# Exchanging the row sums of squares through small SBUF transfers in a fused attention and mixture kernel

## The chip, the cores and the metric

The kernel runs on one core of one Trainium2 chip. The metric is the device time of one execution in microseconds. Three executions of the kernel before took 2057.47, 2061.39 and 2066.37 us; the median is 2061.39 us. The profile was taken on a further execution of 2060.28 us, whose span from the first to the last instruction is 2058.4 us.

## The reference

```python
def _attn_ref(q, k, v):                       # B, H, S, D = 4, 8, 576, 64
    scores = scale * np.matmul(q, k.transpose(0, 1, 3, 2))
    # heads 0..3: the last 32 positions; heads 4..7: every 4th of the last 128
    masks = np.stack([mask_plain if h < H // 2 else mask_dil for h in range(H)], axis=0)
    scores = np.where(masks[None, :, :, :], scores, -1000000000.0)
    ...                                       # softmax over the keys
    return np.matmul(attn, v)

def _moe_ref(x, w_gate, w_val, w_out, rms_g):  # 2304 tokens, 512 -> 1536 -> 512
    rms = np.sqrt(np.mean(x * x, axis=-1, keepdims=True) + 1e-06)
    xn = x / rms * rms_g
    g = xn @ w_gate
    silu = g * (1.0 / (1.0 + np.exp(-g)))
    val = xn @ w_val
    return (silu * val @ w_out)

def _moe2_ref(x, w_gate, w1, w2):              # 8 experts, 512 -> 1024 -> 512
    ...                                       # P: Sinkhorn-normalised gate, 2304 x 8
    for e in range(E):
        h = np.maximum(x @ w1[e], 0.0)
        out += P[:, e:e + 1] * (h @ w2[e])
```

The output of the attention (8 heads of 64) is one row of 512 values per token, and the first step of the second part divides that row by its root mean square.

## The kernel before

**Stages.** The kernel has two phases. In the first (up to about 610 us) the attention and the gated feed-forward layer run together; in the second the eight experts do, with matrix products in which seven block products stand for eight. TensorE works in split precision: every operand is kept as a high and a low part, and each product takes three passes (`PASSES`).

**Attention tiles.** The 2304 tokens are handled in 20 attention tiles of up to 128 tokens, five to a batch. `att_tile` is a generator: it issues a stretch of instructions at each step and yields between them. A tile has the scores (psS), the softmax, a transpose (psT), the product with the values (psX), the scaling into `xf` (named xs in the rows), the sums of squares `ssq`, the normalisation and a last transpose (psXT) from which `xn`, the input of the feed-forward layer, is written as high and low part.

**Two orders of tokens.** Heads 0 to 3 (group 0) use a plain window, heads 4 to 7 (group 1) every fourth position, so in a tile the 128 partitions hold the tokens of the two groups in two orders: partition u of group 1 holds the token that partition `32*(u%4) + u//4` of group 0 holds, counted within each group. A token's row sum needs both halves, so each half sum has to be brought to the other half's partition. In the kernel before two matmuls with permutation matrices (`perms`) do this at L286 into the PSUM tile psR; DVE adds the two halves and 1e-6 into `rstd` (L288), POOL raises it to -0.5 (L289), and DVE scales both halves of the row with it (L291).

**Blocks and pacing.** The feed-forward layer goes by eight blocks of 256 or 320 tokens, each with the tiles of the same tokens (two or three). Per block and chunk, `gemm_h` makes the products pg and pv (L472) and from them h (L484 to L487: ACT, DVE, ACT, POOL), and `gemm_out` the product po (L442), added into `partial` (L451, L453). From block 2 on, `spread` mixes three streams: the products of block i with 34 steps; the attention of block i+1 (`block_att`), for which seven steps per tile are counted; and `weight_sums`, which loads blocks of the experts' weights into three buffers (kbd, vbd, conv; L667), forms sums on POOL and DVE (L680 to L688) and stores them (L690). Tiles 0 to 4 are done earlier with sets of buffers of their own; from tile 5 on `rows` is true, and tiles share one set. Then psT, psR, psXT use one PSUM bank (tag "single").

**Order.** Each engine carries out its own instructions strictly in the order in which a scheduler placed them when the kernel was built; the steps above are hints to it. SP issues nearly all transfers in one such order; ACT issues the loads of q, k and v. Each DMA signals one of eight completion semaphores, taken in turn, and the next user of a semaphore waits until the DMA that had it before has landed.

The lines that the change touches:

Of the kernel before, what the change touches and what calls it, by code (L numbers as in the profile page):

```python
# [7 lines left out]
F32 = mybir.dt.float32  # L8
# [8 lines left out]
P = 128  # L17
# [12 lines left out]
def attention_moe_kernel(  # L30
# [14 lines left out]
    nc = tc.nc  # L45
# [12 lines left out]
    ps_a = psum_a.enter_context(tc.tile_pool(name="ps_a", bufs=3, space=bass.MemoryType.PSUM))  # L58
# [11 lines left out]
    apool = ph1.enter_context(tc.tile_pool(name="apool", bufs=1))  # L70
# [5 lines left out]
    perms = cst[:, C_PM:C_G].rearrange("p (v k) -> p v k", v=2)  # L76
# [78 lines left out]
    def att_tile(n, xn, c0, bufs, after_qk=None, after_pv=None):  # L155
# [4 lines left out]
        rows = bufs.rows  # L160
# [9 lines left out]
        for hp in range(4):  # L170
            for g in range(4):
                off = hp * 160 + 32 * g if hp < 2 else ((hp - 2) * 4 + g) * 64
                if rows:
                    for s in range(2):
# [3 lines left out]
                            lhsT=qs[half, hp, g, :],  # L178
                            rhs=bufs.k[hp // 2][half, 0, off : off + 64],
                            start=True,  # L180
                            stop=True,
# [5 lines left out]
                    lhsT=qs[:, hp, g, :],  # L187
                    rhs=bufs.k[hp // 2][:, :, off : off + 64],
                    start=True,
                    stop=True,  # L190
# [27 lines left out]
        single = dict(tag="single", bufs=1) if rows else dict(tag="a", bufs=3)  # L218
# [15 lines left out]
        for hp in range(4):  # L234
            vals = bufs.v[hp // 2].rearrange("p s (a g d) -> p s a g d", a=2, g=4)
            for g in range(4):
                if rows:
                    for s in range(2):
# [3 lines left out]
                            lhsT=pt[half, hp * 128 + 32 * g : hp * 128 + 32 * g + 32],  # L242
                            rhs=vals[half, 0, hp % 2, g, :],
                            start=True,
                            stop=True,
# [5 lines left out]
                    lhsT=pt[:, hp * 128 + 32 * g : hp * 128 + 32 * g + 32],  # L251
                    rhs=vals[:, :, hp % 2, g, :],
                    start=True,
                    stop=True,
# [20 lines left out]
        ssq = apool.tile([P, 2], F32, tag="ssq", name=f"ssq_{n}", bufs=2)  # L275
# [5 lines left out]
        if after_pv:  # L281
            after_pv()
        yield
        psr = ps_a.tile([P, 512], F32, name=f"psR_{n}", **single)
        for j in range(2):
            nc.tensor.matmul(psr[:, j : j + 1], lhsT=perms[:, j, :], rhs=ssq[:, 1 - j : 2 - j], start=True, stop=True)  # L286
        rstd = apool.tile([P, 2], F32, tag="rstd", name=f"rstd_{n}", bufs=2)
        nc.vector.scalar_tensor_tensor(out=rstd, in0=psr[:, 0:2], scalar=1e-6, in1=ssq, op0=ALU.add, op1=ALU.add)  # L288
        nc.gpsimd.tensor_tensor(out=rstd, in0=rstd, in1=neghalf, op=ALU.pow)  # L289
# [478 lines left out]
    blocks = []  # L768
# [5 lines left out]
    def block_att(i):  # L774
        tok0, n, tl = blocks[i]

        def xn():
            if i not in xns:
                xns[i] = mpool.tile([P, 4, 2, n], F32R, tag=f"xn{i % 2}", name=f"xn_{i}", bufs=1)
            return xns[i]  # L780

        for tn, c0 in tl:
            more = tn + 1 < 20
            yield from att_tile(
                tn, xn, c0, set0,
                (lambda: set0.load_qk(tn + 1, nc.scalar)) if more else None,
                (lambda: set0.load_v(tn + 1, nc.scalar)) if more else None,
            )
# [47 lines left out]
    def some(g, n):  # L836
        for _ in range(n):
            yield next(g, None)

    def tail():  # L840
        for _ in range(9):
            yield
        yield from x_load(0)
        yield from x_split(0)
        yield from first_weights(0)
# [41 lines left out]
    for i in range(2, 8):  # L887
        sides = [(some(sgen1, 24), 24)]
        if i < 7:
            sides.append((block_att(i + 1), 7 * len(blocks[i + 1][2])))  # L890
        else:
            sides += [(tail(), 34)]
        spread(moe1_chunks([(i, 0), (i, 1), (i, 2)]), 34, sides)
# [210 lines left out]
    n = len(units)  # L1104
# [127 lines left out]
```

## Time and profile before

| | |
|---|---|
| median of three executions | 2061.39 us |
| the profiled execution | 2060.28 us |
| its span | 2058.4 us |
| outside the span | 1.9 us |
| PE busy | 2002.0 us (97%) |
| DVE, ACT, POOL busy | 1375.8, 1097.3, 1216.1 us |
| tiles 5 to 19, first and last permutation matmul | 120.2 and 526.7 us |

PE stands for TensorE's matmuls and PEld for its weight loads; DVE is VectorE, ACT ScalarE, POOL GpSimd, and SPq the queue of SyncE, which only issues transfers. A row of a timeline gives the start in the span, the length, the engine, the line and what is written from what; an idle time before it and what ended that stands in brackets. PE is busy almost without a gap, so every instruction on it counts, and what another engine does counts only where PE ends up waiting.

### The profile page before, as it was taken

The numbers are of one execution on the slowest core, as the hardware profiler recorded it, in microseconds if no ns is written. First come the engines' busy times: TensorE is split into PE (matmuls) and PEld (weight loads), VectorE is DVE, ScalarE is ACT, GpSimd is POOL, SyncE is SP. The second block draws the span as 40 slices with busy tenths as digits, with TensorE's granted clock in tenths as the row PEclk, the third lists the DMA queues.
The fourth block names the chain that finished last, engine by engine and source line by source line (L and its number), as shares of the span: only waits on it lengthen the run. The fifth ranks groups of instructions, "written<-read, shape, count | busy, mean of one in ns | idle before, by whom it ended". The sixth has DMA issues, their size and how long they took to land.

```text
span 2058.4 us, 42667 instructions
## 1 busy us (share of the span) xinstructions
PE 2002.0 (97%) x16122; PEld 1966.2 (96%) x16122; DVE 1375.8 (67%) x2890; ACT 1097.3 (53%) x2418; POOL 1216.1 (59%) x1198
## 2 busy tenths in 40 slices
PE   6899999999999999999999999999999999999999
PEld 4788999999998999999999999999999999999999
DVE  7985444434347898778777676776776567667666
ACT  5665443334347666666665555555555654555453
POOL 4786555655647668778776455455545544554452
PEclk9999999999999999999999999999999999999999
DMA  9423767776555678887799656666677666666652
GB/s 271 167 83 113 252 217 240 236 239 225 201 203 211 250 254 283 299 294 265 283 326 352 197 197 227 215 200 226 222 243 266 222 208 200 181 198 205 203 177 81
DMA packets 206557, 459.95 MB, mean 223 GB/s; under 512 B 16784, under 2 KB 56464, under 8 KB 206352
## 3 DMA queue, kind: packets, MB, share of 16 engines
q1 hardware_dynamic: 199296, 438.25, 62.4%
q10 hardware_dynamic: 7056, 18.98, 3.1%
q8 instruction: 127, 2.08, 0.4%
q14 instruction: 78, 0.64, 0.1%
HBM read 344.44 MB, written 112.72 MB: 222 GB/s over the span
## 4 chain that ended last, share of the span: by engine, by line
PE 74%; DMA 7%; DVE 7%; POOL 5%; issue 4%; ACT 2%; SPq 1%; DVEq 0%; POOLq 0%; ACTq 0%
PE ya L1057 17%; PE pa L1004 17%; PE yb L1057 9%; PE pb L1004 9%; PE po L442 4%; PE pc L1004 4%; PE yc L1057 4%; PE pv L472 4%; PE pg L472 4%; DMA kbd<-in_w 1%; DMA sums<-kbd 1%; DMA w0r<-in_w 1%; DMA w0s<-sums 1%; POOL w_s L712 1%; DMA sums<-conv 1%
## 5 line engine op out<-in xcount | busy, mean ns | idle before, releaser
L712 POOL TENSOR_TENSOR w_s<-w0s,w_s 128x512 fp32r<-128x512 f32 x192 | 260.5, 1359 | 92.9 <-ACT w_s L711 91.3
L983 POOL TENSOR_TENSOR h_s<-p,h_s 128x384 fp32r<-128x384 f32 x96 | 104.8, 1113 | 322.6 <-ACT h_s L982 273.7
L1093 DVE SCALAR_TENSOR_TENSOR acc<-ya,Pm,acc 128x256 f32<-128x256 f32 x510 | 221.9, 478 | 65.3 <-PE ya L1057 65.2
L712 POOL TENSOR_TENSOR w_a<-w0r,w_a 128x512 fp32r<-128x512 f32 x144 | 195.3, 1359 | 110.8 <-ACT w_a L711 110.3
L1004 PE MATMUL pa<-x_t,w_s 128*128 128x384 f32 x1152 | 224.1, 336 | 1.9 <-ACT p L1016 1.9
L1057 PE MATMUL ya<-w_t,h_s 128*128 128x256 f32 x1728 | 224.5, 282 | 0.9 <-ACT acc L1082 0.9
L1057 PEld LDWEIGHTS ya<-w_t,h_s 128*128 128x128 f32 x1728 | 218.8, 190 | 1.3 <-ACT acc L1082 1.2
L1004 PEld LDWEIGHTS pa<-x_t,w_s 128*128 128x128 f32 x1152 | 197.1, 188 | 2.5 <-ACT p L1016 2.1
L472 PE MATMUL pv<-xn,w_v 128*128 128x320 f32 (+1 forms) x1152 | 182.2, 301 | 9.7 <-ACT hf L484 2.4
L472 PE MATMUL pg<-xn,w_g 128*128 128x320 f32 (+1 forms) x1152 | 184.2, 301 | 3.2 <-DVE hf L485 1.5
L442 PE MATMUL po<-h,w_o 128*128 128x320 f32 (+1 forms) x1152 | 175.7, 301 | 7.0 <-DVE partial L453 2.4
L472 PEld LDWEIGHTS pv<-xn,w_v 128*128 128x128 f32 x1152 | 162.7, 191 | 14.4 <-ACT hf L484 4.1
L711 ACT CAST w_s<-w0s 128x512 fp32r<-128x512 f32 x192 | 119.8, 625 | 105.4 <-PE pb L1004 65.6
L1093 DVE SCALAR_TENSOR_TENSOR acc<-yb,Pm,acc 128x256 f32<-128x256 f32 x258 | 109.7, 476 | 93.4 <-PE yb L1057 93.3
L442 PEld LDWEIGHTS po<-h,w_o 128*128 128x128 f32 x1152 | 159.8, 190 | 11.2 <-DVE partial L453 3.8
L472 PEld LDWEIGHTS pg<-xn,w_g 128*128 128x128 f32 x1152 | 162.7, 190 | 7.0 <-DVE hf L485 2.3
L487 POOL TENSOR_TENSOR h<-hf,h 128x256 fp32r<-128x256 f32 (+1 forms) x96 | 80.1, 835 | 111.7 <-ACT h L486 111.2
L983 POOL TENSOR_TENSOR h_s<-r,h_s 128x384 fp32r<-128x384 f32 x96 | 96.5, 1028 | 69.1 <-ACT h_s L982 52.9
L1057 PE MATMUL yc<-w_b,h_a 128*128 128x256 f32 x864 | 122.4, 282 | 0.0
L1057 PE MATMUL yb<-w_t,h_s 128*128 128x256 f32 x864 | 121.1, 281 | 0.1
L1057 PE MATMUL yb<-w_t,h_a 128*128 128x256 f32 x864 | 120.2, 282 | 0.0
L711 ACT CAST w_a<-w0r 128x512 fp32r<-128x512 f32 x144 | 89.4, 622 | 56.0 <-DMA w0r<-in_w 15.8
(250 smaller groups left out, 4722.9 us busy)
## 6 DMA issues: line engine op xcount, KB each, us to landing
w_t<-split SPq DMA_DIRECT2D x128, 512.0 KB, 4.3
w0r<-in_w SPq DMA_DIRECT2D x96, 512.0 KB, 6.1
w0s<-sums SPq DMA_DIRECT2D x96, 512.0 KB, 7.3
w_b<-split SPq DMA_DIRECT2D x96, 512.0 KB, 3.9
split<-w_t SPq DMA_DIRECT2D x64, 512.0 KB, 3.0
split<-w_b SPq DMA_DIRECT2D x48, 512.0 KB, 4.0
w1r<-in_w SPq DMA_DIRECT2D x32, 512.0 KB, 5.6
w1s<-sums SPq DMA_DIRECT2D x32, 512.0 KB, 7.6
```

Source lines behind the costliest of these rows:

```text
L442: nc.tensor.matmul(po[:, :n], lhsT=ow[f][:, a, dc * P : dc * P + P], rhs=hs[blk, f][:, bb, :n], start=k == 0, stop=k == 11,)
L472: nc.tensor.matmul(ps[:, :n], lhsT=w[kt, fg][:, a, fo * P : fo * P + P], rhs=xn[:, kt, bb, :n], start=k == 0, stop=k == 11,)
L487: late_g = nc.gpsimd.tensor_tensor(out=h[:, 1, :n], in0=hf, in1=h[:, 0, :n].bitcast(F32), op=ALU.subtract)
L711: nc.scalar.copy(v[:, :, 0, :], src)
L712: lo_eng.tensor_tensor(out=v[:, :, 1, :], in0=src, in1=v[:, :, 0, :].bitcast(F32), op=ALU.subtract)
L983: eng.tensor_tensor(out=h[:, 1, :], in0=src, in1=h[:, 0, :].bitcast(F32), op=ALU.subtract)
L1004: nc.tensor.matmul(ps, lhsT=w1s[u, a][:, kt, hl, q * P : q * P + P], rhs=xc[b, kt][:, xl, :TH], start=fresh and k == 0, stop=k == 5, skip_ ...
L1057: nc.tensor.matmul(ps, lhsT=hh[u, a, q][:, hl, jj * P : jj * P + P], rhs=w2s[u, b][:, q, wl, :], start=fresh and k == 0 and jj != 1, stop= ...
L1093: nc.vector.scalar_tensor_tensor(out=dst, in0=ps, scalar=scale, in1=dst, op0=ALU.mult, op1=ALU.add)
```

## The change

From tile 5 on the two matmuls on PE are left out. In their place a tile `ssx` in SBUF is filled by eight transfers from SP: each carries 32 values of 4 bytes, from every fourth partition to 32 partitions in a row, or back. The addition on DVE reads `ssx` in place of PSUM. `att_tile` yields twice more, so that more of the other streams is placed between the transfers and the addition, and the pacing counts nine steps per tile in place of seven. Tiles 0 to 4 keep the matmuls.

```diff
@@ -281,9 +281,19 @@
         yield
-        psr = ps_a.tile([P, 512], F32, name=f"psR_{n}", **single)
-        for j in range(2):
-            nc.tensor.matmul(psr[:, j : j + 1], lhsT=perms[:, j, :], rhs=ssq[:, 1 - j : 2 - j], start=True, stop=True)
+        if rows:
+            psr = apool.tile([P, 2], F32, tag="ssx", name=f"ssx_{n}", bufs=2)
+            for a in range(4):
+                nc.sync.dma_start(psr[a:P:4, 0:1], ssq[32 * a : 32 * a + 32, 1:2])
+                nc.sync.dma_start(psr[32 * a : 32 * a + 32, 1:2], ssq[a:P:4, 0:1])
+            yield
+            yield
+        else:
+            psr = ps_a.tile([P, 512], F32, name=f"psR_{n}", **single)
+            for j in range(2):
+                nc.tensor.matmul(
+                    psr[:, j : j + 1], lhsT=perms[:, j, :], rhs=ssq[:, 1 - j : 2 - j], start=True, stop=True
+                )
         rstd = apool.tile([P, 2], F32, tag="rstd", name=f"rstd_{n}", bufs=2)
@@ -887,7 +897,7 @@
         if i < 7:
-            sides.append((block_att(i + 1), 7 * len(blocks[i + 1][2])))
+            sides.append((block_att(i + 1), 9 * len(blocks[i + 1][2])))
```

Line numbers after the change are higher by 10 behind the new lines. The order of the instructions differs from the kernel before only in the stretch of tiles 5 to 19. Three places show what moves.

SP while tile 15 is handled, before; DMAHW0 to DMAHW7 are the completion semaphores of transfers, Pool, DVE and Activation those of the engines:

```order
L690 DMA sums_9_103<-kbd 128x1024 [waits DMAHW2_49,Pool_49]
L690 DMA sums_9_103<-vbd 128x1024 [waits DMAHW3_49,Pool_49]
L667 DMA kbd<-in_w 128x2x512 [waits DMAHW2_49]
L667 DMA vbd<-in_w 128x2x512 [waits DMAHW6_49,DMAHW3_49]
L690 DMA sums_9_119<-conv 128x1024 [waits DMAHW7_49,DVE_49,Pool_49]
```

The same place after; L287 and L288 are the eight new transfers of this tile:

```order
L288 DMA ssx_5683<-ssq_5646 32x1 [waits DMAHW3_49,Activation_49]
L288 DMA ssx_5683<-ssq_5646 32x1 [waits DMAHW4_49]
L700 DMA sums_9_103<-kbd 128x1024 [waits DVE_49,Pool_49]
L287 DMA ssx_5683<-ssq_5646 32x1 [waits DMAHW6_49,Activation_49]
L700 DMA sums_9_103<-vbd 128x1024 [waits DMAHW7_49,DVE_49,Pool_49]
L287 DMA ssx_5683<-ssq_5646 32x1 [waits DMAHW0_49]
L287 DMA ssx_5683<-ssq_5646 32x1 [waits DMAHW1_49]
L677 DMA kbd<-in_w 128x2x512 [waits DMAHW5_49,DMAHW2_49]
L288 DMA ssx_5683<-ssq_5646 32x1 [waits DMAHW3_49]
L287 DMA ssx_5683<-ssq_5646 32x1 [waits DMAHW4_49]
L288 DMA ssx_5683<-ssq_5646 32x1
L700 DMA sums_9_119<-conv 128x1024 [waits DMAHW6_49,DVE_49,Pool_49]
```

The stores of the weight sums and the next load of kbd now stand behind transfers that wait for ACT's sums of squares of tile 15, and three of the eight transfers stand behind the load.

PE at the start of block 3 (tile 9 is the last of its tokens), before:

```order
L442 MATMUL po_2_3_3665<-h_11_3509,w_o_1886 128x256 x3
L286 MATMUL psR_3327<-ssq_3300,cst 128x1 x2
L176 MATMUL psS_3535<-kbd,q_3227 32x64 x32
L604 MATMUL pl_3759<-xn_2200,wg 16x256 x7
L297 MATMUL psXT_3370<-cst,xs_3298 128x128 x4
L604 MATMUL pl_3759<-xn_2200,wg 16x256
L472 MATMUL pg_0_3515<-xn_2793,w_g_383 128x320
```

The same place after:

```order
L452 MATMUL po_2_3_3695<-h_11_3539,w_o_1886 128x256 x3
L176 MATMUL psS_3565<-kbd,q_3251 32x64 x32
L614 MATMUL pl_3798<-xn_2206,wg 16x256 x8
L641 MATMUL ptl_3890<-id_83,lg_3845 128x16 x2
L641 MATMUL ptl_3890<-id_83,lg_3845 64x16
L307 MATMUL psXT_3419<-cst,xs_3305 128x128 x4
L482 MATMUL pg_0_3545<-xn_2811,w_g_383 128x320
```

The permutation is gone, and the last transpose of the tile still stands directly ahead of the first product of the block, with one more matmul of the gate and its small transposes (ptl) ahead of it.

PE at the start of block 5 (tile 14 is the last of its tokens), before:

```order
L297 MATMUL psXT_5234<-cst,xs_5168 128x128 x4
L472 MATMUL pg_10_5314<-xn_3881,w_g_1719 128x256
L472 MATMUL pg_10_5314<-xn_3881,w_g_1738 128x256 x3
...
L472 MATMUL pv_11_5348<-xn_3881,w_v_1812 128x256 x3
L472 MATMUL pg_0_5379<-xn_4677,w_g_383 128x320 x3
```

The same place after:

```order
L482 MATMUL pv_11_5408<-xn_3935,w_v_1812 128x256 x3
L176 MATMUL psS_5459<-kbd,q_5153 32x64 x32
L452 MATMUL po_2_0_5522<-h_8_5240,w_o_1830 128x256 x2
...
L452 MATMUL po_2_3_5589<-h_11_5433,w_o_1886 128x256 x3
L307 MATMUL psXT_5313<-cst,xs_5207 128x128 x4
L614 MATMUL pl_5692<-xn_3935,wg 16x256 x6
L482 MATMUL pg_0_5439<-xn_4725,w_g_383 128x320
```

The last transpose moved from 40 matmuls ahead of the block's first product to only the gate's six ahead of it, and 47 of the 48 matmuls of po were pulled in front of both. The start of block 7 (tile 19) changed in nearly the same way.

## Rows read from the trace of the kernel before

**Rows 1.** The page: its first line and PE's busy time.

```profile
span 2058.4 us, 42667 instructions
PE 2002.0 (97%) x16122; PEld 1966.2 (96%) x16122; DVE 1375.8 (67%) x2890; ACT 1097.3 (53%) x2418; POOL 1216.1 (59%) x1198
```

**Rows 2.** Busy times by stretch: length, PE, PEld, DVE, ACT, POOL, clock, DMA.

```profile
110.00:560.00 450.00, 438.52 (x4896) 421.00 (x4895) 220.99 (x472) 192.21 (x442) 283.62 (x384) 1.00 0.61 204
300.00:350.00 50.00, 49.88 (x526) 48.26 (x526) 17.79 (x39) 17.75 (x40) 28.64 (x38) 1.00 0.72 241
```

**Rows 3.** PE's waits, 110 to 560 us: total us, times, longest.

```profile
PE psXT L297 <- DVE xs L291: 2.5, 4, 0.9
PE po L442 <- DVE partial L453: 2.4, 3, 1.3
...
PE po L442 <- POOL h L487: 0.3, 1, 0.3
```

**Rows 4.** The tile psR, 110 to 560 us: ns min/median/max.

```profile
L286 PEld LDWEIGHTS psR<-ssq,cst x60: 187/192/193, 120.1 to 526.7; 128*128 128x128 f32 x60
L286 PE MATMUL psR<-ssq,cst x60: 166/250/250, 120.2 to 526.7; 128*128 128x1 f32 x60
```

**Rows 5.** Timeline at the permutation of tile 19: start, length.

```profile
526.32 0.53 PEld L286 LDWEIGHTS psR<-ssq,cst 128*128 128x128 f32 x4
...
526.78 0.30 PEld L442 LDWEIGHTS po<-h,w_o 128*128 128x128 f32 x2
```

**Rows 6.** Timeline of SP, two runs of three transfers: start, length.

```profile
998.71 1.29 SPq L548 DMA_DIRECT2D xr<-x2d  x3
...
938.00 2.24 SPq L548 DMA_DIRECT2D xr<-x2d  x3
```

**Rows 7.** DMA issues in short windows: KB, median us from issue to landing.

```profile
x2d<-partial SPq DMA_DIRECT2D x1, 160.0 KB, 1.8
...
sums<-kbd SPq DMA_DIRECT2D x1, 512.0 KB, 5.1
x2d<-partial SPq DMA_DIRECT2D x1, 160.0 KB, 4.8
...
id<-in_consts SPq DMA_DIRECT2D x1, 1.0 KB, 3.0
...
sums<-conv SPq DMA_DIRECT2D x1, 512.0 KB, 4.5
```

**Rows 8.** Timelines at the start of block 3, with tile 9.

```profile
262.47 0.34 SPq L690 DMA_DIRECT2D sums<-conv  x1
...
262.49 0.19 ACT L278 ACTIVATION_READ_ACCUMULATOR psX<-xs 128x1 f32 x1
...
265.39 0.16 DVE L288 SCALAR_TENSOR_TENSOR rstd<-psR,ssq 128x2 f32<-128x2 f32 x1
...
267.33 0.63 PE L297 MATMUL psXT<-cst,xs 128*128 128x128 f32 x4 [0.34 <-DVE xs L291]
...
268.31 0.42 PE L472 MATMUL pg<-xn,w_g 128*128 128x320 f32 x1 [0.24 <-ACT xn L307]
```

**Rows 9.** Timeline of PE ahead of block 5, with tile 14.

```profile
394.52 0.60 PE L297 MATMUL psXT<-cst,xs 128*128 128x128 f32 x4
...
399.76 1.92 PE L472 MATMUL pg<-xn,w_g 128*128 128x320 f32 x12
```

**Rows 10.** POOL's waits for transfers, 300 to 350 us: total us, times, longest.

```profile
POOL vbd L685 <- DMA vbd<-in_w: 3.6, 1, 3.6
```

**Rows 11.** Timelines of SP, ACT and POOL while tile 15 is handled.

```profile
412.70 0.38 SPq L690 DMA_DIRECT2D sums<-kbd  x1
...
415.86 0.38 SPq L667 DMA_DIRECT2D kbd<-in_w  x1
...
417.83 0.44 ACT L484 ACTIVATE hf<-pg 128x320 f32<-128x320 f32 x1 [0.97 <-PE pg L472]
...
425.48 0.72 POOL L685 TENSOR_TENSOR kbd<-kbd 128x256 f32<-128x256 f32 x1
```

## The prediction

> **What bounds the kernel now.** I read the page first: PE is busy for 2002.0 of 2058.4 us, so over the whole program PE is the bound [rows 1]. The change reaches tiles 5 to 19 only, so the busy times of that stretch come next: between 110 and 560 us PE is busy for 438.52 of 450 us [rows 2]. PE idles there for 11.5 us in all, and that is everything that better timing could win beside the work taken off PE itself. The waits of PE in that stretch name its parts: the last transpose of a tile, psXT, waits for the scaling on DVE 4 times for 2.5 us together; po waits 2.4 us for the adding on DVE; for h from POOL it waits only 0.3 us [rows 3]. The other engines have room on average: DVE is busy for 221 and POOL for 284 of the 450 us [rows 2]. How late they may be before PE feels it is told by one wait: between 300 and 350 us POOL stood 3.6 us waiting for a load of vbd [rows 10], and PE still was busy for 49.88 of 50 us [rows 2].
>
> **What is removed.** There are 60 weight loads and 60 matmuls of psR for 15 tiles, so four pairs per tile [rows 4]. Their durations (192 and 250 ns) overlap, so I don't add them up; I take the distance by which they hold up the stream. At tile 19 the first weight load of psR starts at 526.32 and the next weight load of po at 526.78 [rows 5]: 0.46 us. For 15 tiles that is 15 x 0.46 = 6.9 us, all on PE, where nothing hides it. This term is the surest. A second gain comes with the new order: psXT of tiles 7, 12 and 17 now stands among the products of a later f, some 5 us of matmuls further back. Of the 2.5 us for which psXT waited [rows 3], 0.34 us belong to tile 9 [rows 8] and stay; the other three waits, 2.2 us, go. Together 9.1 us.
>
> **What is added on SP.** Eight transfers per tile, 120 in all. Issuing them takes time on SP: three transfers of xr in a row took 1.29 us, and in another place 2.24 us [rows 6], so 0.43 to 0.75 us each, and 3.4 to 6.0 us for eight. No transfer as small as these 128 bytes stands in the trace. Their landing I bound by others: 1.8 us for 160 KB with nothing ahead of it, 4.8 us for the same 160 KB issued 0.4 us behind a store of 512 KB that itself took 5.1 us, and 3.0 us for 1 KB in the early, busy stretch [rows 7]. From the sums of squares to the last landing that makes 5.2 us (3.4 + 1.8) to 10.8 us (6.0 + 4.8). I take 7 us, nearer to the low end: the issues nearest in kind are the quick ones, and the landing near 3 us is that of the smallest transfer.
>
> The second pair in these rows also shows that a small transfer does not overtake a large one that was issued just ahead of it: it landed with it. The Trainium skill says the same (DMA: Bandwidth & Descriptors, Queues, rings and completion order): on each DMA engine the descriptors of one queue are consumed in the order of the ring. By that rule alone every tile whose transfers stand directly behind a load of 512 KB would be at the long end for landing; the trace agrees in its one pair. The same page (Anatomy of one DMA) puts the fixed cost of a transfer at about 2 us, whatever its size; eight in a row overlap it, so by that figure the estimate would be 3.4 + 2.0 = 5.4 us. No run here shows it for 128 bytes.
>
> **Where this is late: PE.** In most tiles the new order leaves room: two yields more put several products between the sums and the addition. The starts of blocks 3, 5 and 7 are the exceptions, since the first product there needs the last tile's psXT.
>
> Block 3, tile 9: ACT ends the sums of squares at 262.68 (262.49 + 0.19), and the addition ran at 265.39; from it to psXT took 1.94 us [rows 8]. With 7 us the addition comes at about 269.7, 4.3 us later than before. The two ends give 2.5 and 8.1 us. Part of this is covered: the gate's matmul and its small transposes that now precede psXT, and what PE had been waiting there anyway (0.34 and 0.24 us) come to about 0.8 us. The store of conv ahead, issued at 262.47 and 4.5 us in landing [rows 7, 8], also holds a completion semaphore that one of the last two transfers needs, so before 267.0 they can't all be issued; the low end is therefore no likelier than the middle. I take 3.5 us of PE idle, with 1.7 to 7.3 as the ends.
>
> Blocks 5 and 7, tiles 14 and 19: before, psXT ran 5.2 us ahead of the block's first product (394.52 against 399.76) [rows 9], so that ACT's and DVE's work behind it was hidden. Now it is not: I charge 1 us each, the distance from psXT to the first product in block 3 (268.31 - 267.33) [rows 8]. In front of it stand the matmuls of po with two PSUM buffers, and the addition for rstd stands ahead of the first adding of po on DVE; a DVE that waits for the transfers therefore holds the third po up. I charge 1.5 us each for that, between nothing and 3 us. Both together: 5 us, ends 2 and 8.
>
> **Where this is late: DVE, POOL and SP.** Elsewhere DVE, which can't pass the waiting addition, stands still for up to some 3 us; behind it are hf and partial, and PE waits for these in the end. The 3.6 us of POOL's wait that PE did not feel [rows 2, 10] are the measure: I cost a stall up to this size at nothing. On SP the transfers stand ahead of stores and loads of the weight sums. The worst place is tile 15: the store of kbd went out at 412.70; now it stands behind two transfers that need sums of squares made around ACT's hf at 417.83, so it leaves 5 to 6 us later, and so does the load of kbd (before at 415.86), which waits for the store's landing. From that load's issue to POOL's use of it at 425.48 lie 9.6 us [rows 11]; with a landing of 4.5 to 5.1 us, as such transfers took [rows 7], some 4.8 us of it are room, so POOL starts about 1 us late, still below the 3.6 us [rows 10]. Tile 10 has the same pattern with less delay. For the partly hidden stalls of tiles 8, 10, 11, 13, 15, 16 and 18 I charge 0.4 us each, 3 us; the ends are 0 and 2 us each, 14 us. In tile 5 the transfers stand ahead of five loads of weights, on which ACT starts only when it is through with the blocks of weights before them; I cost this at nothing, and at up to the 3.4 to 6.0 us of the eight issues if that cover is gone.
>
> **The sum.** -6.9 - 2.2 + 3.5 + 5 + 3 = +2.4 us. On the profiled execution of 2060.28 us (span 2058.4 us and 1.9 us around it, which do not change) this is 2062.7 us. That execution stood 1.1 us below the median of 2061.39 us, so I predict **2063 us**. All low ends together (1.7 + 2 + 0) give -5.4, all high ends (7.3 + 8 + 14) +20.2, that is 2056 to 2082 us.
>
> **Rivals.** First, *the transfers are hidden everywhere* and only the gain is left: -9.1 us, 2052 us. For it speaks the slack of PE against late engines [rows 2, 10]; against it that psXT of tile 9 stands directly ahead of the block's first product, and that even 5.2 us are 2.5 us too long there. It also cannot reach much further down, for the idle time of the stretch is 11.5 us and most of it has nothing to do with this change.
>
> Second, *SP becomes the bound of the weight sums* (slower). Its place is SP's order: eight issues and their waits for semaphores delay the load that follows by 3.4 to 6.0 us at each tile, and POOL already stands waiting for such loads. It decides from the point where POOL is held up by more than the 3.6 us that PE did not feel. Then h comes late, and PE waits at po for POOL, which it did for 0.3 us only [rows 3]. If the 13 tiles from 7 on each cost PE 2 us beyond the gain, the sum is 13 x 2 - 9.1 + 3.5 = +20 us, 2082 us. For it: SP issues everything in one order, and the transfers at the long end need 10.8 us. Against it: the weight sums are only needed in the second phase, and each wait that PE does not feel costs nothing.
>
> Third, *the saved PE time is not real*, because PE waits at the same places anyway: the gain is then about nothing, and the cost of block starts stays, +11 us, 2073 us. Against it: PE waits for 11.5 us in this stretch, mostly not near a permutation.
>
> **How the numbers follow.** This kernel's executions differ by about 0.25% either way, and changes of up to 0.5% (10.3 us, so 2051.1 to 2071.7 us) can't be told from none. The forecast case, 2056 to 2071 us, gets 0.57; the hidden case 0.13, half of which may be measured below 2051 us; SP as the bound 0.24 and the lost saving 0.06, which lie above 2071.7 us except for a few hundredths. So faster 0.07, same 0.62, slower 0.31. The range for 8 in 10 is 2053 to 2083 us; it leaves out a good part of the hidden case and the far end of the second rival. The likeliest case's own range is 2056 to 2071 us.
>
> **What the profile after would show.** The psR rows from tile 5 on are gone and PE's matmuls are fewer by 60. SP shows eight issues per tile, in 3.4 to 6.0 us where nothing else stands between them, and a landing near 3 us. At the start of block 3 PE idles 3 to 4 us ahead of psXT and its first product; at the starts of blocks 5 and 7 PE idles about 2 us each. PE's waits for psXT at tiles 7, 12 and 17 are gone, and po's wait for h from POOL stays below 3 us. I am wrong on the side of too slow if psXT of tile 9 comes without a gap, and on the other if PE's waits for h and hf grow to 10 us or more, or if an issue of a 128-byte transfer takes over 0.75 us.

## The result and the profile after

The changed kernel takes 2090.34 us (median of 4 runs, 2088.14 to 2092.18) against 2061.4 us of the kernel before beside it: ratio 1.0145, interval 1.0129 to 1.016, some 29 us slower. I had predicted 2063 us with a range of 2053 to 2083, so the time lies outside the range. A per cent is 20.6 us here; where a run below is given in us against the kernel before, it is its ratio times that.

The page after, its first line and PE's busy time, answers to [rows 1]:

```profile
span 2089.1 us, 42738 instructions
PE 2011.3 (96%) x16062; PEld 1974.2 (95%) x16062; DVE 1385.8 (66%) x2890; ACT 1097.6 (53%) x2418; POOL 1216.7 (58%) x1198
```

The span grew by 30.7 us. PE has 60 matmuls fewer and is still busy 9.3 us longer; its idle time grew by the other 21.4 us. If the removed matmuls took the 6.9 us that I charged, the remaining work took 16 us longer than before in this trace. Both parts lie in the stretch of [rows 2]; the columns are the same (length, PE, PEld, DVE, ACT, POOL, granted clock, DMA):

```profile
110.00:560.00 450.00, 417.99 (x4651) 399.18 (x4634) 213.16 (x449) 183.90 (x420) 264.22 (x358) 0.96 0.58 193
300.00:350.00 50.00, 49.32 (x512) 47.95 (x511) 18.35 (x38) 16.03 (x34) 28.54 (x38) 1.00 0.73 240
```

PE's busy time over 450 us fell from 438.52 to 417.99 us, and the mean granted clock from 1.00 to 0.96. The second row shows that it is not so everywhere: from 300 to 350 us, the block of two tiles, PE is busy for 49.32 of 50 us, against 49.88 before.

PE's waits in that stretch (total us, times, longest), answering to [rows 3], and DVE's first wait:

```profile
PE psXT L307 <- DVE xs L301: 13.9, 8, 4.2
PE ptl L641 <- ACT lg L634: 3.2, 1, 3.2
PE po L452 <- DVE partial L463: 3.0, 2, 2.2
PE psS L176 <- ACT psX L278: 2.7, 1, 2.7
...
PE po L452 <- ACT h L496: 1.8, 1, 1.8
PE pv L482 <- ACT hf L494: 1.8, 2, 1.5
...
PE po L452 <- POOL h L497: 0.4, 1, 0.4
```

```profile
DVE rstd L298 <- DMA ssx<-ssq: 49.2, 12, 7.3
```

The largest new wait is that of psXT, 13.9 us against 2.5, and behind it stands DVE: the addition for rstd waits 12 times for the transfers, 49.2 us in all. PE's wait for h from POOL, the sign of my rival of SP as the bound, is 0.4 us against 0.3 before.

The transfers by themselves (ns of an issue min/median/max; the last row is us from issue to landing):

```profile
L288 SPq DMA_DIRECT2D ssx<-ssq x60: 492/592/1373, 117.7 to 565.2; - x60
L287 SPq DMA_DIRECT2D ssx<-ssq x60: 469/592/1522, 119.7 to 564.5; - x60
DMA to landing us min/median/max: 1.6/3.0/7.0
```

An issue takes 0.59 us and a landing 3.0 us, both as I had assumed. What was longer is the way from the sums to the last landing. The timeline of ACT, SP and DVE at tile 13 is the longest of them:

```profile
388.74 0.19 ACT L278 ACTIVATION_READ_ACCUMULATOR psX<-xs 128x1 f32 x1
...
397.02 0.36 ACTq L125 DMA_DIRECT2D q<-in_qt  x1
...
397.91 0.40 ACT L496 CAST h<-hf 128x256 fp32r<-128x256 f32 x1 [7.68 <-DMA ssx<-ssq]
```

```profile
393.33 0.38 SPq L677 DMA_DIRECT2D vbd<-in_w  x1
393.81 0.50 SPq L288 DMA_DIRECT2D ssx<-ssq  x1
...
398.18 0.59 SPq L288 DMA_DIRECT2D ssx<-ssq  x1
```

```profile
SPq L677 <- DMA sums<-vbd: 5.7, 1, 5.7
```

The sums are there at 388.93, but SP stands at a load of vbd ahead of the transfers until 393.33: for 5.7 us it waits until the store from the same buffer has landed (the single row, SP's waits from 386 to 400 us). Its eight issues then end at 398.77, and DVE's addition runs at 401.49: 12.6 us behind the sums. In the 12 tiles in which DVE waited it was 6.8 to 12.6 us, 9.5 at the median, worked out in the same way from the same rows of each tile. ACT stands here too, for 6.8 us ahead of the load of q for the next tile. That load leaves at 397.02, and the completion semaphore for which ACT stood belongs to SP's load of vbd, which landed at 396.94; only the load of kbd behind it waits for a small transfer (landed at 397.39), which the bracket names since it came last. With both loads ACT idles 7.68 us ahead of h.

DVE's addition at tiles 10, 11, 12, 13, 15 and 17 (the wait stands in the brackets):

```profile
306.10 0.16 DVE L298 SCALAR_TENSOR_TENSOR rstd<-ssx,ssq 128x2 f32<-128x2 f32 x1 [4.68 <-DMA ssx<-ssq]
332.78 0.16 DVE L298 SCALAR_TENSOR_TENSOR rstd<-ssx,ssq 128x2 f32<-128x2 f32 x1 [2.71 <-DMA ssx<-ssq]
373.63 0.16 DVE L298 SCALAR_TENSOR_TENSOR rstd<-ssx,ssq 128x2 f32<-128x2 f32 x1 [6.57 <-DMA ssx<-ssq]
401.49 0.16 DVE L298 SCALAR_TENSOR_TENSOR rstd<-ssx,ssq 128x2 f32<-128x2 f32 x1 [7.29 <-DMA ssx<-ssq]
454.30 0.16 DVE L298 SCALAR_TENSOR_TENSOR rstd<-ssx,ssq 128x2 f32<-128x2 f32 x1 [4.18 <-DMA ssx<-ssq]
522.32 0.16 DVE L298 SCALAR_TENSOR_TENSOR rstd<-ssx,ssq 128x2 f32<-128x2 f32 x1 [7.00 <-DMA ssx<-ssq]
```

Tiles 10, 11 and 15 are of blocks of two: DVE stands for 2.7 to 4.7 us and PE goes on with at most 0.7 us of gaps near them. Tiles 12, 13 and 17 are of blocks of three: DVE stands for 6.6 to 7.3 us, and PE feels it, at tile 17 for instance with 3.00 us ahead of psXT.

What follows such a gap is the second part of the loss. PE at the start of block 3, which answers to [rows 8]:

```profile
271.58 1.34 PE L614 MATMUL pl<-xn,wg 128*16 128x256 f32 x8
276.15 0.33 PE L641 MATMUL ptl<-id,lg 16*128 16x16 f32 x3 [3.23 <-ACT lg L634]
280.73 1.11 PE L307 MATMUL psXT<-cst,xs 128*128 128x128 f32 x4 [4.25 <-DVE xs L301]
...
282.89 1.80 PE L482 MATMUL pg<-xn,w_g 128*128 128x320 f32 x6
...
287.57 1.04 PE L482 MATMUL pg<-xn,w_g 128*128 128x320 f32 x6
```

```profile
277.00:287.00 10.00, 5.92 (x22) 5.52 (x23) 2.42 (x8) 1.68 (x4) 0.70 (x1) 0.51 0.35 121
```

PE stood for 7.5 us in two gaps. From 277 to 287 us the granted clock is 0.51, the lower of the two levels (1.2 GHz): six products of pg take 1.80 us there, and 1.04 us later. Six more such stretches, 27 us in all, stand between 110 and 560 us, and each begins during a gap of PE or within 1.4 us after one; the 2.24 us of gap ahead of psXT at tile 7 are followed by none. The kernel before has no such stretch there [rows 2].

### The profile page after: what moved, and what is told of

It is laid out like the page before. It is cut to its first block, busy times and chain, and to the rows that moved or that the text cites. A ratio compares the mean times of both kernels' runs of the same rounds, so it can differ in the third digit from the quotient of the medians.

```text
span 2089.1 us, 42738 instructions
## 1 busy us (share of the span) xinstructions
PE 2011.3 (96%) x16062; PEld 1974.2 (95%) x16062; DVE 1385.8 (66%) x2890; ACT 1097.6 (53%) x2418; POOL 1216.7 (58%) x1198
## 4 chain that ended last, share of the span: by engine, by line
PE 73%; DMA 8%; DVE 8%; POOL 4%; issue 3%; ACT 2%; SPq 2%; DVEq 0%; ACTq 0%; POOLq 0%
PE ya L1067 17%; PE pa L1014 17%; PE yb L1067 9%; PE pb L1014 9%; PE yc L1067 4%; PE pc L1014 4%; PE po L452 4%; PE pg L482 3%; PE pv L482 3%; DMA w0r<-in_w 2%; DMA ssx<-ssq 1%; DMA sums<-kbd 1%; SPq L287 1%; DMA kbd<-in_w 1%; POOL w_s L722 1%
## 5 line engine op out<-in xcount | busy, mean ns | idle before, releaser
L482 PE MATMUL pv<-xn,w_v 128*128 128x320 f32 (+1 forms) x1152 | 187.4, 305 | 10.5 <-ACT hf L494 3.3
L452 PE MATMUL po<-h,w_o 128*128 128x320 f32 (+1 forms) x1152 | 181.8, 308 | 9.4 <-DVE partial L463 3.5
L452 PEld LDWEIGHTS po<-h,w_o 128*128 128x128 f32 x1152 | 165.8, 198 | 13.3 <-DVE partial L463 4.6
```

Source lines behind the costliest of these rows:

```text
L452: nc.tensor.matmul(po[:, :n], lhsT=ow[f][:, a, dc * P : dc * P + P], rhs=hs[blk, f][:, bb, :n], start=k == 0, stop=k == 11,)
L482: nc.tensor.matmul(ps[:, :n], lhsT=w[kt, fg][:, a, fo * P : fo * P + P], rhs=xn[:, kt, bb, :n], start=k == 0, stop=k == 11,)
```

## The experiments

Two theories to begin with. **Waiting**: what costs is that DVE and then PE wait for the result of the transfers, and the clock falls behind these waits. **Queue**: what costs is that SP issues 120 transfers more and that they share queues and completion semaphores with the loads, whoever reads the result. A third, **order**: the new places of the instructions cost time by themselves. All edits are against the changed kernel.

**One part alone.** The matmuls in the new order:

```diff
-            for a in range(4): ...   # the eight transfers into psr
             yield
             yield
-        else:
-            psr = ps_a.tile(...)      # the permutation matmuls
+        psr = ps_a.tile(...)          # the permutation matmuls, for every tile
```

> Tiles 5 to 19 use the permutation matmuls again, but behind the two extra yields and with nine steps per tile: the new order without the transfers. Waiting theory (the addition waits for the transfers, PE idles ahead of psXT and is then granted half its clock): the order costs nothing, 2058 to 2064 us, and the granted clock between 100 and 600 us is 1.0. Order theory (the later places of psXT and of the yields cost time by themselves): 2070 us or more, with PE's waits for psXT near the 14.1 us of the changed kernel.

Measured: ratio 1.0 (0.9985 to 1.0015). The yields and steps cost nothing beyond the 3 us of the interval; the granted clock from 110 to 560 us is 0.99. The order theory is out only for them. Counted in products of the feed-forward layer (pg, pv, po) that PE runs before it, psXT of tiles 7, 12 and 14 stands behind 936, 1801 and 2072 in the kernel before, behind 948, 1812 and 2080 here, and behind 977, 1838 and 2160 in the changed kernel. The places of the changed kernel come with the waiting for the transfers, and no run has them without it.

Neither transfers nor matmuls (`psr = ssq` in their place):

> Leaves out the exchange: from tile 5 on each group's own sum of squares stands in for the other group's; no transfer, no permutation matmul; yields and steps as in the changed kernel. If the 0.46 us per tile that I took off PE is real, the time is 15 x 0.46 = 6.9 us below the kernel before, about 2 us more if the waits of psXT go, so 2052 to 2056 us. If PE's saved time turns up again as waits elsewhere: 2059 to 2063 us.

Measured: 0.9974 (0.996 to 0.9988), 5.4 us faster than before. With this order it is all that could be won; my term of 6.9 us lies inside the interval (2.5 to 8.2 us), the 9.1 us that I summed up do not.

The transfers issued, the matmuls used:

```diff
-            psr = apool.tile([P, 2], F32, tag="ssx", ...)
+            ssx = apool.tile([P, 2], F32, tag="ssx", ...)
             ...                       # the eight transfers, now into ssx
-        else:
-            psr = ps_a.tile(...)
+        psr = ps_a.tile(...)          # the matmuls, behind the two yields
```

> The eight transfers per tile are issued as in the changed kernel, but nothing reads what they bring: the permutation matmuls give the sums, behind the two yields. Waiting theory: what costs is the waiting for the result, so 2060 to 2068 us, and the clock stays at 1.0 but for a stretch or two. Queue theory (eight issues on SP, and the completion semaphores that they share with the loads on SP and ACT, hold up loads, weight sums and ACT whoever reads the result): 2080 us or more. Of the 21.4 us by which PE's idle time grew, 10 us stand ahead of instructions other than psXT (psS 2.7, ptl 3.2, pv 1.5, po 1.8 and 2.2); if these come from the queue alone and the rest from the waiting, the time lies between, at 2070 to 2080 us.

Measured: 1.0053 (1.0036 to 1.007), 10.9 us, between the two theories. The transfers cost about a third of the loss even where nothing reads what they bring.

**By place.** The condition `if rows` ahead of the transfers narrowed, first to the blocks of two tiles, then to those of three, then to the last tiles of the blocks of three:

```diff
-        if rows:
+        if rows and n in (5, 6, 10, 11, 15, 16):     # second: not in; third: in (9, 14, 19)
```

> Transfers in the blocks of two tiles only (tiles 5, 6, 10, 11, 15 and 16), permutation matmuls in the blocks of three; yields and steps as in the changed kernel everywhere. Waiting theory by place: in the changed kernel's trace PE's long gaps (2.2 us and more) stand at tiles 7, 8, 9, 12, 14 and 17, all in blocks of three, so the six tiles cost nothing and save 6 x 0.46 = 2.8 us: 2056 to 2062 us. If every tile with transfers costs alike, 6/15 of the 29 us are left: 2070 to 2075 us.

> The complement of the run with two-tile blocks: transfers at tiles 7, 8, 9, 12, 13, 14, 17, 18 and 19, permutation matmuls at 5, 6, 10, 11, 15 and 16. If the cost has its place in the blocks of three tiles, all of it is here: 2086 to 2095 us. If the two runs do not add up (the cost comes from tiles in a row), the time is 2070 to 2080 us.

> Transfers only at the last tiles of the blocks of three: 9, 14 and 19. My prediction charged these block starts 3.5 + 5 us; less 3 x 0.46 us of matmuls that is 2068 us. By the changed kernel's trace: at tile 9 the idle time grew by 7 us and the half clock cost 3 us, at tile 14 it is 2.2 and 1.6 us, at tile 19 nothing: 14 us, less 1.4, 2074 us. If the block starts are not where the cost arises: 2058 to 2063 us.

Measured: 1.0002 (0.9987 to 1.0018) for the blocks of two, 1.0161 (1.0135 to 1.0187) for the blocks of three, 1.0036 (1.0023 to 1.0049) for the last tiles. All of the loss has its place in the blocks of three, 33 us, and the two runs add up to that of the changed kernel within their intervals. The last tiles account for 7.4 us; tiles 7, 8, 12, 13, 17 and 18 for the difference, 26 us, which no run measured by itself. In the run with the last tiles PE's long wait is at tile 9:

```profile
265.85 0.33 PE L644 MATMUL ptl<-id,lg 16*128 16x16 f32 x3 [0.56 <-ACT lg L637]
270.88 1.12 PE L310 MATMUL psXT<-cst,xs 128*128 128x128 f32 x4 [4.70 <-DVE xs L304]
```

How long DVE may stand differs too. Tile 15 in the run with the blocks of two, then tile 7 (a block of three) in the changed kernel:

```profile
424.65 0.16 DVE L301 SCALAR_TENSOR_TENSOR rstd<-ssx,ssq 128x2 f32<-128x2 f32 x1 [6.21 <-DMA ssx<-ssq]
426.13 0.63 PE L310 MATMUL psXT<-cst,xs 128*128 128x128 f32 x4 [0.83 <-DVE xs L304]
```

```profile
218.95 0.16 DVE L298 SCALAR_TENSOR_TENSOR rstd<-ssx,ssq 128x2 f32<-128x2 f32 x1 [6.43 <-DMA ssx<-ssq]
220.34 0.70 PE L307 MATMUL psXT<-cst,xs 128*128 128x128 f32 x4 [2.24 <-DVE xs L301]
```

Nearly the same standing of DVE costs PE 0.83 us in the one and 2.24 us in the other.

**Fewer transfers.** Two of 128 rows instead of eight, which leaves out the permutation:

```diff
-            for a in range(4):
-                nc.sync.dma_start(psr[a:P:4, 0:1], ssq[32 * a : 32 * a + 32, 1:2])
-                nc.sync.dma_start(psr[32 * a : 32 * a + 32, 1:2], ssq[a:P:4, 0:1])
+            nc.sync.dma_start(psr[:, 0:1], ssq[:, 1:2])
+            nc.sync.dma_start(psr[:, 1:2], ssq[:, 0:1])
```

> Two transfers of 128x4 B per tile instead of eight of 32x4 B; leaves out the permutation (each group gets the other's sum of the same row). Everything else as in the changed kernel, whose eight issues end 5.2 to 9.8 us behind the sums of squares because each takes a completion semaphore in turn and waits for that semaphore's earlier transfer. Number theory: with two, issue and landing end some 4 us behind the sums (2 x 0.5 and a landing of 3 us) instead of 9, PE's idle time and the half clock mostly go, and the time is 2056 to 2066 us. Landing theory (the one landing, not the number, is what is waited for): 2075 us or more, with psXT still waiting 2 us and more at tiles 7, 9, 12 and 17.

Measured: 1.0116 (1.009 to 1.0142), 24 us. The number theory fell. Of the other theory the total holds, but not every place: psXT waits 4.4 us at tile 12 and 2.4 us at tile 17, 0.6 us at tile 9 and nothing at tile 7. DVE's and PE's waits, 110 to 560 us, and the transfers (KB each, median us to landing):

```profile
DVE rstd L297 <- DMA ssx<-ssq: 48.9, 13, 7.3
...
PE psXT L306 <- DVE xs L300: 11.8, 8, 4.4
```

```profile
ssx<-ssq SPq DMA_DIRECT2D x30, 0.5 KB, 4.5
```

A transfer of 128 rows takes 4.5 us to land instead of 3.0. From the sums to the addition it is 6.9 us at the median instead of 9.5 (tiles with a wait), and yet DVE waits as long as before, 48.9 us. The way without the wait shows why: in the changed kernel DVE came to the addition 5.3 us behind the sums, here 2.8 us (median of the way less the wait): the new order puts the addition forward by as much as was won. That it does so because the planner reckons two transfers shorter than eight is my reading; the two medians are measured.

**More and fewer yields.** Four yields with eleven steps per tile, and none with seven:

```diff
-            yield
-            yield
+            yield                      # four times, or not at all
...
-            sides.append((block_att(i + 1), 9 * len(blocks[i + 1][2])))
+            sides.append((block_att(i + 1), 11 * len(blocks[i + 1][2])))   # or 7 *
```

> Four yields instead of two behind the transfers, and eleven steps per tile instead of nine. Hiding theory (more yields give the transfers more cover): the waits of psXT at tiles 7, 12 and 17 (7.8 us of idle time, and half clock behind two of them) shrink: 2075 to 2083 us. Planner theory (psXT stands where the planner reckons the transfers to have landed, however many yields there are, and the chip is later than the reckoning): the rows of psXT are nearly the same, and so is the time, 2085 to 2095 us.

> The eight transfers alone: no yields added, seven steps per tile as in the kernel before. If the yields and steps are worth something, this is slower than the changed kernel by 5 us or more, 2095 us and up; if the planner sets the places anyway, 2086 to 2095 us like the changed kernel.

Measured: 2096 us with four, ratio 1.0164 (1.0133 to 1.0195), and 2086 us with none, 1.0103 (1.0078 to 1.0128). Both lie within 2 us of the planner theory's ranges, and psXT of tiles 7, 12 and 17 stands within ten products of its place in the changed kernel in either order. What neither theory says is that none are faster than two; between two and four the intervals overlap. The yields hide nothing, and the first two cost a little. Why they cost is not settled.

**Other queues.** Two transfers on ACT's queue, all eight on GpSimd's, and all eight on ACT's (`nc.scalar` or `nc.gpsimd` in the place of `nc.sync` in the lines above):

> The two transfers of 128x4 B (no permutation, as in the run before with two) on ACT's queue instead of SP's. On SP's queue they were issued up to 5 us behind the sums, since SP stood at an earlier store, and landed 1.2 us behind the issue where nothing was ahead (tile 5), but 5 us behind it where loads of 512 KB had just been issued (tile 9). Queue-order theory: issued by ACT right behind its own sums and in a queue with no large load ahead, they land within some 3 us of the sums at every tile; DVE's waits go, and the time is 2055 to 2068 us. Shared-engine theory (the large transfers occupy the DMA engines whatever the queue, and the completion semaphores are shared): landings of 4 us and more remain, ACT itself now waits, and the time is 2080 us or more.

> The eight transfers are issued on GpSimd's queue, whose eight completion semaphores no load uses; SP then issues only loads and stores. Semaphore theory: the issues no longer wait for loads of 512 KB, SP and ACT are not held up, and what is left is the latency of the transfers: 2070 to 2080 us if an issue on GpSimd takes about 1 us or less (no row shows it yet). If GpSimd's issues hold up its own work (h, weight sums) by more than that, the time is 2085 us or more, and PE's waits stand at po for h.

> The eight transfers on ACT's queue, the full exchange. With two the move to ACT's queue brought the loss from 24 us to 9 us. If the queue decides, eight cost ACT some 4 us of issuing per tile more and the time is 2070 to 2080 us, below the changed kernel; if ACT's issues and its waits for completion semaphores hold up hf and h, it is 2090 us or more.

Measured: 1.0043 (1.0029 to 1.0057) with two on ACT, 15 us less than with two on SP; 1.0192 (1.0165 to 1.0219) with eight on GpSimd; 1.0264 (1.0248 to 1.028) with eight on ACT. The waits and the transfers of the first:

```profile
DVE rstd L297 <- DMA ssx<-ssq: 32.6, 12, 5.7
...
PE psXT L306 <- DVE xs L300: 7.2, 7, 2.4
```

```profile
ssx<-ssq ACTq DMA_DIRECT2D x30, 0.5 KB, 4.7
```

The landing is no shorter in ACT's queue, 4.7 us; that half of the queue-order theory fell. I had expected ACT's queue to be free of large loads, and it is not: at 13 tiles the load of v (512 KB) is under way in it. But at tiles 8 and 19, where nothing in the queue was under way, the landings took 4.1 to 5.1 us, while SP's loads and stores were under way; and at tile 10, with such a load 1.3 us ahead in the same queue and nothing from SP, they took 1.7 and 2.0 us. What is won is the issue: ACT issues right behind its own sums, at 13 of 15 tiles within 1.5 us of them, where SP took up to 5.7 us. With eight, ACT itself stands at the issues:

```profile
ACT h L496 <- DMA ssx<-ssq: 61.7, 9, 10.9
```

On GpSimd an issue takes 0.54 us and PE's longest gaps (8.5 and 8.3 us) are longer than on SP; I expected 2070 to 2080 us if issues were that quick, and 2085 us or more with PE's waits at po for h otherwise. The time is of the second kind, but these waits are 0.5 us. Semaphores of their own do not pay for the transfers by themselves.

**Waiting against queue, directly.** Each tile uses what the transfers of the tile before it brought:

```diff
             yield
             yield
+            psr, stale["ssx"] = stale.get("ssx", ssq), psr
```

(`ssx` has three buffers here instead of two.)

> The eight transfers as in the changed kernel, no permutation matmul, but each tile uses what the transfers of the tile before it brought (tile 5 its own sums), so that nothing waits for a transfer just issued; the exchanged sums are therefore those of another tile. Waiting theory: what is left is the cost of the eight issues on SP and their completion semaphores (10.9 us in the run with unused transfers) less the 5.4 us of the matmuls: 2062 to 2069 us, so that 20 us and more of the changed kernel's loss are the waiting for the result. Queue theory: 2080 us or more.

Measured: 1.0042 (1.0021 to 1.0063), 8.7 us, just above the upper end of the waiting theory. Without the waiting 21 of the 30 us come back. The run doesn't take away the waiting alone: psXT of tiles 7, 12 and 14 stands behind 942, 1803 and 2064 products again, so the new places went with it. What is left is the queue, 8.7 us although the 5.4 us of the matmuls are saved, so 14 us; the run with unused transfers gives 10.9, within the intervals the same. PE now waits in another place, and POOL ahead of it:

```profile
PE po L455 <- POOL h L500: 5.3, 3, 3.2
PE psXT L310 <- DVE xs L304: 3.9, 4, 1.3
```

```profile
385.39 0.72 POOL L698 TENSOR_TENSOR vbd<-vbd 128x256 f32<-128x256 f32 x1 [5.18 <-DMA vbd<-in_w]
```

This is the mechanism of my second rival: POOL waits for the loads of kbd, vbd and conv for 42 us here (from 110 to 560 us) against 20 in the kernel before, and behind the longest of these waits, 5.18 us, h comes late and PE stands for 3.2 us at po. In the changed kernel POOL's waits for these loads are 12.5 us, and it does not show.

The loads of q, k and v on SP's queue, in the changed kernel and, as a control, in the kernel before:

```diff
-                (lambda: set0.load_qk(tn + 1, nc.scalar)) if more else None,
-                (lambda: set0.load_v(tn + 1, nc.scalar)) if more else None,
+                (lambda: set0.load_qk(tn + 1, nc.sync)) if more else None,
+                (lambda: set0.load_v(tn + 1, nc.sync)) if more else None,
```

> The changed kernel with the loads of q, k and v for the next tile on SP's queue instead of ACT's. In the changed kernel's trace ACT stands for 16.7 us at such loads, whose completion semaphore belongs to one of the small transfers not yet landed (6.8 us of it at tile 13, where PE then waits 1.5 and 1.8 us). If this coupling costs, ACT's waits go and the ratio to the control (the kernel before with its loads on SP too) is smaller than 1.0145 by 0.3% or more; if not, the ratio stays at 1.012 to 1.017.

> The control: the kernel before with the loads of q, k and v on SP's queue. It waits behind SP's stores, so 2060 to 2070 us.

Measured: 1.015 (1.0127 to 1.0173) and 0.9981 (0.997 to 0.9992). The loss is as large as with the loads on ACT, so ACT's standing at its loads, visible as it is at tile 13, is not what decides. (The 6.8 us there end with SP's load of vbd, not with a small transfer, as I had read them.) The control, for which I had expected 2060 to 2070 us, is the one version here with the whole exchange that beats both kernels, by 4 us, and has nothing to do with the change.

**The clock.** Redundant matmuls on PE around ptl of block 2:

```diff
+        for _ in range(18 if blk == 2 else 0):       # ahead of ptl's transposes; 26 behind them
+            nc.tensor.matmul(ptl[:16, 256 : 256 + n], lhsT=wg[:, 0]..., rhs=xns[blk][:, 0, 0, :n], start=True, stop=True)
```

> The changed kernel, with 44 redundant matmuls (16x256, their results unused) around ptl of block 2, where PE idled 3.2 and 4.3 us ahead of block 3; PE's order is else the same. If the half clock there (10.2 us from 276.9) is the answer to that idling, no stretch of half clock stands between 265 and 300 us, and the time falls by half of the 6.6 us of it in which PE had work, 3 us: 2087 us against 2090. If the half clock has another cause, the stretch stays, and the time is 2090 us or more.

Measured: 1.0156 (1.0129 to 1.0182), 2091 us. PE there, and the stretch from 265 to 300 us in this run; the changed kernel has the granted clock 0.85 in it:

```profile
276.46 0.33 PE L643 MATMUL ptl<-id,lg 16*128 16x16 f32 x3 [2.83 <-ACT lg L634]
276.71 3.15 PE L646 MATMUL ptl<-xn,wg 128*16 128x256 f32 x26
280.13 0.70 PE L307 MATMUL psXT<-cst,xs 128*128 128x128 f32 x4 [0.27 <-DVE xs L301]
281.19 0.42 PE L482 MATMUL pg<-xn,w_g 128*128 128x320 f32 x1 [0.35 <-ACT xn L317]
...
281.59 1.04 PE L482 MATMUL pg<-xn,w_g 128*128 128x320 f32 x6
```

```profile
265.00:300.00 35.00, 31.55 (x404) 28.65 (x403) 12.35 (x29) 12.46 (x29) 15.55 (x21) 1.00 0.47 147
```

With PE working until psXT the clock stays at 2.4 GHz, and the six products of pg take 1.04 us at once. So the half clock here was the answer to PE's standing. The expected 3 us do not show in the total: this run has waits elsewhere that are longer (po at 418 us for 4.5 us), and 3 us are less than the interval either way.

How much of a trace lies at half clock does not fix the total. In the changed kernel 37.5 us do between 110 and 560 us, and PE works in 31.6 of them, so they cost some 16 us. In the run with the loads on SP, just as slow, only 17.1 us do, with 10.0 us of work, some 5 us; there PE stands longer instead, 83.4 us of the span against 77.8:

```profile
span 2086.3 us, 42740 instructions
PE 2002.9 (96%) x16062; PEld 1965.4 (94%) x16062; DVE 1381.3 (66%) x2890; ACT 1094.7 (52%) x2418; POOL 1215.8 (58%) x1198
```

## Why the prediction was wrong

**The matmuls, -6.9 us: right within the measurement** (-5.4, from -8.2 to -2.5).

**The waits of psXT at tiles 7, 12 and 17, -2.2 us: wrong in sign.** I read psXT's later place as cover. I take it to be where the planner reckons the transfers to have landed, and the chip is later. PE waits 2.2 us at tile 7, 2.5 at tile 12 and 3.0 at tile 17. The runs bear this out as far as they go: other numbers of yields leave the place within ten products, and where nothing waits for the transfers psXT stands 26 to 35 products earlier.

**Issue and landing, 3.4 to 6.0 and about 3 us: right each, but the sum of 7 us was too small** (9.5 at the median, up to 12.6 against my upper end of 10.8). I added the issues to the landing as if SP came free with the sums; it stands at loads and stores first, and each issue waits for the completion semaphore it takes. I had used that wait only for tile 9. The fixed 2 us that I took from the Trainium skill (DMA: Bandwidth & Descriptors, Anatomy of one DMA) are given there for transfers that GpSimd issues; those took 4.3 us at the median here, and SP's 3.0.

**The starts of blocks 3, 5 and 7, +8.5 us: right as a sum, by luck in its parts.** The run with the last tiles alone gives 7.4 us, and 1.4 us of saved matmuls on top, so 8.8. In it tile 9 alone has a long gap (4.7 us, and half clock behind it), tiles 14 and 19 have none. In the changed kernel tile 9 costs 7.5 us of gaps against the 0.6 us of before, since ptl waits too.

**Tiles 8, 10, 11, 13, 15, 16 and 18, +3 us: this is the step that failed.** I let DVE stand for up to some 3 us and costed a stall up to 3.6 us at nothing. That measure was one wait of POOL between 300 and 350 us, in a block of two. For the blocks of two it held: DVE's waits up to 4.7 us were not felt. In the blocks of three they are up to 7.3 us, and the six tiles 7, 8, 12, 13, 17 and 18 cost 26 us by the difference of two runs. The prediction's bounds for this term, up to 2 us for a tile, were too narrow for them: one late addition keeps DVE from hf and partial, ACT from h and lg, PE waits in several places, and then can pay at half clock.

**SP's delay of the loads: at nearly nothing.** I let POOL start about 1 us late at tile 15 and charged no more. The transfers by themselves cost 11 to 14 us.

**The clock: no term at all.** The kernel before shows 1.00 through this stretch, so no row of it carried the price. After, 37.5 us at half clock lie between 110 and 560 us, and PE's remaining work took about 16 us longer in this trace; other traces as slow have less of it.

**The rivals.** The number of the second, 2082 us, was the nearest, but not by its mechanism: PE's wait for h stayed at 0.4 us. It is there, hidden, and shows with 5.3 us once the waiting is gone. My own signs of being too fast (waits for h and hf of 10 us, an issue over 0.75 us at the median) both did not come: I was wrong by a third way, the late addition in the middle of the blocks, with 7.7 us of waits at psXT of tiles 7, 12 and 17 as its plainest part.

The sum itself should have been 2063.8 us (2061.4 + 2.4), not 2063; nothing hangs on it.

The sum by the runs: 5.4 us gained on PE, 11 to 14 us lost by the queue, and the other 21 to 24 us lost by the waiting, with the new places and the clock behind it; together 30 us. How these divide into standing and half clock in time, and not in the trace, is open: the one run on it gave back nothing measurable. So is whether the new places cost anything beyond the waits.

## What to carry to other kernels

Where a planner sets the order, an instruction that has moved back need not be cover: it may stand only where the planner reckons its input to be ready, and what is left as a wait is the chip's time beyond the reckoning (49 us for DVE with eight transfers as with two). A tiny operation that waits for a transfer on an engine that works in order stops all that is behind it; ask how long the engine may stand before the bound engine feels it, by stage, since a block of three tiles bore less than one of two. And where the bound engine is TensorE, a gap can cost more than its length, since the products behind it may run at half clock.

## What the runs showed of the hardware

- A transfer of 32x4 B took 1.6 to 7.0 us to land (median 3.0), one of 128x4 B 4.5 us, and 4.7 us on ACT's queue. The Trainium skill (DMA: Bandwidth & Descriptors, Issuing engines are not separate DMA queues) says that transfers run on the same DMA engines whoever starts them; the two medians agree. My sentence on small transfers behind large ones in one queue names too narrow a cause: on ACT's queue they took 4.1 to 5.1 us with nothing under way in the queue and SP's loads beside them, and 1.7 and 2.0 us behind a load of 512 KB with nothing from SP.
- A load issued by ACT can stand until a transfer of SP has landed whose completion semaphore it takes over (6.8 us between ACT's hf and its load of q at tile 13 of the changed kernel, until SP's load of vbd, 512 KB, had landed).
- Between 110 and 560 us of the changed kernel half clock followed gaps of PE of 1.8 to 7.5 us, but not the one of 2.2 us at tile 7; a gap of 2.8 us in the run with redundant matmuls was followed by none.
